# An attention and state-space kernel on one core: the row maxima of the loop turned by VectorE's 32x32 blocks in place of a TensorE transpose

## The chip, the cores and the metric

The kernel runs on one core of a Trainium2 chip. TensorE (PE) multiplies, VectorE (DVE), ScalarE (ACT) and GpSimd (POOL) work element by element, SyncE (SP) issues DMAs. The metric is the device time of one execution in microseconds, the median over runs.

## The reference, cut to what matters

Two independent heads are computed in float32 and put side by side. Head A is a long convolution (a kernel made of 256 complex exponentials per channel, applied through Fourier transforms). Head B is full softmax attention with 16 heads of 28 channels over 2048 positions:

```python
x = inputs["B_x"]            # (1, 2048, 448); u has the same shape
qkv = (x @ wqkv).reshape(B, S, 3, H, Dh).transpose(2, 0, 3, 1, 4)
scores = einsum("bhqd,bhkd->bhqk", q, k) * Dh ** -0.5
o = einsum("bhqk,bhkd->bhqd", softmax(scores), v)
b = o.transpose(0, 2, 1, 3).reshape(B, S, D) @ wo
a = irfft(rfft(u, 2L) * rfft(K, 2L))[:L] + u * D_skip   # K = 2 Re sum_n C exp(A dt l)
return concatenate([a, b], -1)
```

## The kernel before, in words

Attention works in 16 rows: row u is one group of four heads (`g = u // 4`) and one chunk of 512 queries (`c = u % 4`). A row has 16 key tiles of 128 keys; one key tile is one step of the loop (lines 1061 to 1118), 256 steps in all. The softmax needs each query's maximum before its exponentials, so a row's maxima are computed a row and three steps ahead (`LEAD`): while step s multiplies, exponentiates and sums row u, it also makes four products (`m0` to `m3`, function `max_mm`) for the maxima of the next row. DVE reduces them from PSUM into `mx`; for one of the four, ACT first makes `rl` and DVE adds and reduces in one custom operation.

The maximum enters the scores as two more channels of q. The tile `qhat` holds q with every channel on four partitions (high and low parts), and K has ones in its channels 28 and 29 (`kones`). When the sixteenth step of a row's maxima is done, `max_join` reduces `mx` to `m1`, 128 queries by 16 numbers (4 heads by 4 tiles of 128 queries). `max_end` (lines 214 to 220) splits them into minus the maximum rounded to fp32r and the rest, `max_put` (222 to 225) writes them by DMA into partitions 112 and 116 of `qhat`. Since `m1` has queries on partitions and the row in `qhat` has them along one partition, they have to be turned: `nc.tensor.transpose` does so into a PSUM tile `pm`, and the pair of DVE operations reads it there as 16 partitions of 128.

The order in which a step's work is written is a table, `ORDER` (line 35); every engine executes its own instructions in the order written. Letters `m` and `s` are products for the maxima and for the scores, `pv` the sums with V, `v` one DVE operation of head A, `k` head A's kernel blocks, `f` a slot. There are two slots a step (three at the end), one before `pv` and one behind it; each takes the first job that is due: urgent ones (`soon_slot`), then the others: `u_stage1` and `u_stage2` (products `ua`), blocks of head A's kernel (`e,g` and `w,ko`), spectra (`yk,mw` and `p,mw`), the last transform (`zi,wb`), output projections (`ua,og`). The turn of a row's maxima is an urgent job, due two slots after the join (line 1116). All these jobs and the products for the maxima share three PSUM tiles `pm` in a ring: the next user of a tile waits until DVE or ACT has emptied it.

GpSimd's work in the loop is `e_power` (lines 689 to 701): per block of head A nine products or sums on SBUF tiles `e`, `eu`, `sdb`, in three sizes. DVE's own share, `g_powers` (703 to 726), keeps one operand `zg` in PSUM. SP issues all DMAs of the loop, in the order written.

Row 0's maxima are made before the loop in a stage of their own (lines 603 to 605).

Of the kernel before, what the change touches and what calls it, by code (L numbers as in the profile page):

```python
# [21 lines left out]
DH = 28  # L22
G = 4
HG = H // G
CQ = 512
NQ = L // CQ
NK = L // 128
# [13 lines left out]
UG = (2, 2, 4)  # L41
# [51 lines left out]
def body(ctx, tc, a, out):  # L93
    nc = Engines(tc)
# [23 lines left out]
    ident = const.tile([128, 128], F32, name="ident")  # L118
# [37 lines left out]
    def load_v(g, c):  # L156
        v_g[g, c] = t = v_p.tile([128, NK // NQ, HG, 32], F32, name="v", bufs=5)
        nc.sync.dma_start(t.rearrange("p t h e -> p t (h e)"), v_d[c][:, g])

    def load_kd(g, j, rows=range(4)):  # L160
        if 0 in rows:
            kd_g[g, j] = kd_p.tile([128, CQ], F32R, name=f"kdif{j}")
        t = kd_g[g, j]
        for r in rows:
            nc.sync.dma_start(t[r::4].bitcast(F32), kd_d[g][r % 2, 32 * j:32 * j + 32, :])

    def load_q(u, rows=range(4)):
        g, c = divmod(u, NQ)
        if 0 in rows:
            q_u[u] = q_p.tile([128, HG, CQ], F32R, name="qhat", bufs=3)  # L170
        t = q_u[u]
        for r in rows:
            nc.sync.dma_start(t[r::4].bitcast(F32), q_d[g][c][r // 2].rearrange("(j p) q -> p j q", j=HG))
# [36 lines left out]
    def max_join(u, n=3):  # L210
        m_u[u, 1] = q_p.tile([128, HG * 4], F32, name="m1", bufs=2)
        nc.vector.tensor_reduce(m_u[u, 1], m_u[u].rearrange("p a b c -> p (a b) c")[:, :, :n], axis=AX.X, op=ALU.max)

    def max_end(u, ps):
        nc.tensor.transpose(ps[:16, :128], m_u[u, 1], ident)
        mh = q_p.tile([16, 2, 128], F32R, name="mh")
        nc.vector.tensor_scalar(mh[:, 0, :], ps[:16, :128], -1.0, None, op0=ALU.mult)
        nc.vector.scalar_tensor_tensor(mh[:, 1, :], ps[:16, :128], -1.0, mh[:, 0, :].bitcast(F32),
                                       op0=ALU.mult, op1=ALU.subtract)
        mh_u[u] = mh  # L220

    def max_put(u, queue=nc.sync):
        for i in range(2):
            queue.dma_start(q_u[u][4 * (DH + i):4 * (DH + i) + 1, :, :].rearrange("p h (t q) -> p (h t) q", t=4).bitcast(F32),
                                mh_u[u][:, i, :].bitcast(F32))


    with ExitStack() as st:
        sst, xst, wst = ExitStack(), ExitStack(), ExitStack()
# [5 lines left out]
        ps_t = pool(st, "ps_t", 2, PSUM)  # L235
# [25 lines left out]
        t = a["A_log_dt"]  # L261
# [51 lines left out]
        for s in (1, 0, 2):  # L313
            for k in range(NCK):
                for p in range(1 if k < NCK - 1 else 2):
                    n = CK if k < NCK - 1 else TL
# [284 lines left out]
        nc.scalar.activation(half_pi[:1], half_pi[:1], AF.Exp)  # L601
        n_st.close()
        max_join(0, 2)
        max_end(0, ps_t.tile([128, CQ], F32, name="pt"))
        max_put(0, nc.scalar)
        sst.close()


# [160 lines left out]
    def s_mm(u, kt, j):  # L769
        pss = ps_s.tile([128, CQ], F32, name="pss")  # L770
        nc.tensor.matmul(pss, kt_g[u // NQ][j][:, kt * 128:(kt + 1) * 128], q_u[u][:, j, :], start=True, stop=True)
        p = kq_p.tile([128, CQ], F32, name="p", bufs=PB)
        nc.scalar.activation(p, pss, AF.Exp, scale=SCALE)
        return p
# [10 lines left out]
    def load_og(u):  # L785
        og_u[u] = og = kq_p.tile([128, G - 1, CQ], F32, name="og")
        nc.sync.dma_start(og, on_d[u % NQ][:G - 1].rearrange("g p q -> p g q"))
# [217 lines left out]
    def soon_slot(gap, f):  # L1005
        n_urgent[0] += 1
        urgent.append((n_slot[0] + gap, n_urgent[0], f))
        q = sorted(urgent)
        urgent.clear()
        urgent.extend(q)  # L1010

    def slot(s_):
        n_slot[0] += 1
        if urgent and urgent[0][0] <= n_slot[0]:
            urgent.popleft()[2]()
        elif s_ >= NS and f_slot(s_, "s"):
            pass
        elif p_due and p_due[0][0] <= s_:
            p_due.popleft()[1]()
        elif m_due and m_due[0][0] <= s_:  # L1020
            m_due.popleft()[1]()
        elif u_due and u_due[0][0] <= s_:
            u_part(*u_due.popleft()[1:])
        else:
            f_slot(s_, "s") or f_slot(s_, "f")

    def k_seed(s_):
        b = k_due[0] if k_due else NB
        if b < NB and b not in egs and done["mm"] >= b - 2 and K0 + b * KP <= s_ + (1 if b in es else 2):
            k_seeds(b)  # L1030
# [30 lines left out]
    for s in range(NS):  # L1061
        u, kt = divmod(s, NK)
        sm = s + NK + LEAD
        if s == 12 * NK:
            k0_st.close()
            f_p["s", 0] = f_p["s", 1] = pool(f0_st, "f0_p", side="right")
            f_ready["s", 0], f_ready["s", 1] = s, NS
        if s >= 12 * NK and f_ready["s", 1] == NS and not (k_due or m_due or powers["g"] or powers["e"]):
            g_st.close()
            ps_st.close()  # L1070
            ps_w[:] = pool(ps_st, "ps_f", 4, PSUM), 1
            f_ready["s", 1] = s + F1
        if kt == 12 and u // NQ == G - 1:
            load_og(u)
        late[0] = s + NK + LEAD > NS
        if u % NQ == NQ - 1 and u < NU - 1 and kt % 4 == 2:
            load_v(u // NQ + 1, kt // 4)
        if sm < NS and sm // NK % NQ == NQ - 1 and sm % NK % 4 == 0 and sm % NK and sm // (NQ * NK) + 1 < G:
            load_kd(sm // (NQ * NK) + 1, sm % NK // 4 - 1)
        if sm < NS and sm % (NQ * NK) == 0 and sm:  # L1080
            load_kd(sm // (NQ * NK), HG - 1)
        if kt % 4 == 1 and u % NQ == 1 and u // NQ + 1 < G:
            load_k(u // NQ + 1, kt // 4, k_pools[(u // NQ + 1) % 2])
        if kt == 2:
            if u + 2 < NU:
                load_q(u + 2)
        ps = []
        for op in ORDER:
            if op[0] == "s":
                ps.append(s_mm(u, kt, int(op[1])))  # L1090
            elif op[0] == "f":
                slot(s)
            elif op[0] == "v":
                vec()
            elif op == "k":
                k_next()
                k_begin(s)
                k_seed(s)
                for _ in range(3):
                    if powers["e"]:  # L1100
                        powers["e"].popleft()()
            elif op == "pv":
                if prev:
                    pv_step(*prev)
                    if prev[1] == NK - 1:
                        fin(prev[0], s)
            elif sm < NS:
                max_mm(sm // NK, sm % NK, int(op[1]))
        for _ in range(FX if late[0] else 0):
            slot(s)  # L1110
        if sm < NS and sm % NK == NK - 1:
            def end(un=sm // NK):
                max_end(un, w_tile())
                max_put(un)
            max_join(sm // NK)
            soon_slot(UG[0], end)
        k_next()
        prev = (u, kt, ps)
    pv_step(*prev)
# [65 lines left out]
```

## Time and profile before

| what | us |
|---|---|
| median of 3 runs | 1278.05 (1277.69 to 1278.42) |
| the profiled execution | 1278.83 |
| its span, first to last instruction | 1277.0 |
| PE busy | 1216.2 |
| ACT busy | 967.0 |
| DVE busy | 922.6 |
| POOL busy | 843.6 |

A row of a timeline gives the start and the length in us, the engine, the operation, what it writes and reads, its shape, and in brackets how long the engine had been idle and who ended that. A group's row gives a count, the busy time and the mean in ns, then the idle time before it. All lines stand as L77, a helper through which every operation is recorded, so tiles tell them apart: `pm` and `pss` are PSUM tiles, `po` the sums with V, `mh` the split maxima. The loop lies between about 230 and 1252 us.

### The profile page before, as it was taken

Reading aid. Unit: us, or ns where it says so; the run is one execution under the profiler, and the core shown is the slowest. Engines: PE = TensorE matmul, PEld = TensorE weight load, DVE = VectorE, ACT = ScalarE, POOL = GpSimd, SP = SyncE. Lnnn points to the kernel's source line nnn. Section 1 sums busy time; section 2 is a strip of 40 time slices with the busy share of each in tenths; the row PEclk is TensorE's granted clock in tenths of the full one; section 3 lists DMA queues with packets and bytes.
Section 4 is the critical chain, followed back from the end, with each engine's and each line's share of the span. In section 5 each row is a group of like instructions: output and inputs, shape, how many; then the busy total and the mean of one; then the engine's idle time right before and its main releaser. Section 6 shows DMA issues by size and latency. Waiting matters only on the chain.

```text
span 1277.0 us, 33251 instructions
## 1 busy us (share of the span) xinstructions
PE 1216.2 (95%) x12593; PEld 692.5 (54%) x12593; DVE 922.6 (72%) x2106; ACT 967.0 (76%) x2162; POOL 843.6 (66%) x728
## 2 busy tenths in 40 slices
PE   6788888999999999999999999999999999999998
PEld 4666764555555555555555555555555555544433
DVE  5788966877777877778778988888887645645111
ACT  5888865788888888888888888888887656656552
POOL 2666740798788888878689999989995222324321
PEclk9999898899999999999999999999999999999999
DMA  6678789436554645475533133432224533657656
GB/s 194 211 258 290 275 278 359 124 88 187 159 154 114 169 118 159 123 224 177 171 101 96 57 80 105 145 91 71 83 60 149 171 139 135 205 162 237 203 163 174
DMA packets 203528, 206.22 MB, mean 161 GB/s; under 512 B 98344, under 2 KB 162408, under 8 KB 201320
## 3 DMA queue, kind: packets, MB, share of 16 engines
q1 hardware_dynamic: 202840, 203.50, 51.8%
q8 instruction: 99, 1.62, 0.5%
q10 hardware_dynamic: 528, 0.59, 0.2%
q14 instruction: 61, 0.50, 0.1%
HBM read 121.60 MB, written 82.18 MB: 160 GB/s over the span
## 4 chain that ended last, share of the span: by engine, by line
PE 79%; DVE 9%; ACT 5%; issue 3%; POOL 2%; DMA 1%; SPq 1%; ACTq 0%; POOLq 0%; DVEq 0%
PE pm L77 44%; PE pss L77 17%; PE po L77 17%; DVE tri L77 1%; ACT tri L77 1%; DVE mx L77 1%; DVE sg L77 1%; SPq L77 1%; ACT rl L77 1%; DVE hl L77 1%; DVE px L77 1%; ACT p L77 1%; PE pt L77 1%; POOL p L77 1%; DVE g L77 1%
## 5 line engine op out<-in xcount | busy, mean ns | idle before, releaser
L77 ACT ACTIVATE p<-pss 128x512 f32<-128x512 f32 x1024 | 561.3, 611 | 111.5 <-PE pss L77 108.4
L77 PE MATMUL pss<-qhat,khat 128*128 128x512 f32 x1024 | 402.8, 399 | 1.5 <-ACT p L77 1.4
L77 DVE TENSOR_REDUCE mx<-pm 128x1 f32<-128x512 f32 x480 | 308.3, 683 | 108.9 <-PE pm L77 106.8
L77 PE MATMUL pm<-khat,qhat 128*128 128x512 f32 x749 | 326.3, 439 | 6.6 <-ACT rl L77 4.4
L77 POOL TENSOR_TENSOR e<-e,sdb 128x256 f32<-128x256 f32 x168 | 201.8, 1201 | 111.4 <-ACT e L77 62.2
L77 PE MATMUL po<-p,v 128*32 128x512 f32 x2048 | 269.1, 594 | 0.0
L77 POOL TENSOR_TENSOR e<-e,eu 128x256 f32<-128x256 f32 x168 | 248.1, 1477 | 13.2
L77 PEld LDWEIGHTS pm<-khat,qhat 128*128 128x128 f32 x749 | 141.2, 189 | 202.8 <-ACT p L77 46.9
L77 DVE CUSTOM_DVE_ANT_0 rl<-pm,rl 128x512 f32<-128x512 f32 x259 | 178.2, 688 | 73.7 <-ACT rl L77 70.8
L77 PEld LDWEIGHTS pss<-qhat,khat 128*128 128x128 f32 x1024 | 190.4, 188 | 46.1 <-issue 10.8
L77 POOL TENSOR_TENSOR eu<-e,sdb 128x256 f32<-128x256 f32 x168 | 201.9, 1202 | 0.0
L77 POOL TENSOR_TENSOR p<-pr,pr 64x448 f32<-64x448 f32 x64 | 73.1, 1142 | 161.4 <-PE pm L77 134.7
L77 ACT ACTIVATE rl<-pm 128x512 f32<-128x512 f32 x259 | 156.8, 607 | 15.4 <-PE pm L77 9.4
L77 DVE TENSOR_TENSOR g<-g,zg 128x128 f32<-128x128 f32 x392 | 161.9, 413 | 3.4
L77 PE MATMUL pm<-kdif,qhat 128*128 128x512 f32 x249 | 100.9, 405 | 6.0 <-DVE xn L77 4.1
L77 PE MATMUL pm<-xh,khat 128*128 128x512 f32 x256 | 85.0, 423 | 12.1 <-DVE hl L77 5.3
L77 DVE TENSOR_TENSOR zg<-g,zg 128x128 f32<-128x128 f32 x224 | 88.0, 393 | 5.0
L77 PEld LDWEIGHTS pm<-e,g 128*32 128x32 f32 x3584 | 57.2, 109 | 43.9 <-issue 16.2
L77 DVE TENSOR_TENSOR pr<-pm,ub 128x448 f32<-128x448 f32 x64 | 37.0, 619 | 56.4 <-PE pm L77 42.0
L77 PE MATMUL pm<-e,g 128*32 128x64 f32 x3584 | 73.0, 222 | 1.9 <-POOL e L77 1.3
L77 ACT ACTIVATE y<-pm 128x448 f32<-128x448 f32 x48 | 26.5, 553 | 58.2 <-PE pm L77 35.9
L77 ACT ACTIVATE ub<-pm 128x224 f32<-128x224 f32 (+1 forms) x96 | 38.7, 448 | 39.5 <-PE pm L77 37.4
(135 smaller groups left out, 1436.7 us busy)
## 6 DMA issues: line engine op xcount, KB each, us to landing
sdb<-sd SPq DMA_DIRECT2D x55, 336.0 KB
qhat<-q SPq DMA_DIRECT2D x64, 256.0 KB
khat<-k SPq DMA_DIRECT2D x64, 256.0 KB
sd<-sg SPq DMA_DIRECT2D x8, 1456.0 KB
k<-hl SPq DMA_DIRECT2D x16, 512.0 KB
mw<-in_mw SPq DMA_DIRECT2D x16, 512.0 KB
sd<-qhat SPq DMA_DIRECT2D x8, 896.0 KB
yu_d<-ub SPq DMA_DIRECT2D x64, 112.0 KB
```

The source lines that it names most:

```text
L77: i = f(*args, **kw)
```

## The change

`max_end` no longer uses TensorE. Straight behind the join, DVE takes the rounded negative and the rest on `m1` as it lies, 128 partitions by 16 (into `mh`, now an SBUF tile of 128 by 2 by 16), and then turns that tile of 128 by 32 with its own transpose, which turns each block of 32 partitions by 32 elements by itself (into `mt`). In `mt`, 32 partitions hold the two parts of 16 numbers for 32 queries, so `max_put` needs four requests, one for each block, with pieces of 32 elements, in place of two with pieces of 128. The urgent job is gone from the slots. Row 0 keeps the old way (`max_first`).

```diff
-    def max_end(u, ps):
-        nc.tensor.transpose(ps[:16, :128], m_u[u, 1], ident)
-        mh = q_p.tile([16, 2, 128], F32R, name="mh")
-        nc.vector.tensor_scalar(mh[:, 0, :], ps[:16, :128], -1.0, None, op0=ALU.mult)
-        nc.vector.scalar_tensor_tensor(mh[:, 1, :], ps[:16, :128], -1.0, mh[:, 0, :].bitcast(F32),
-                                       op0=ALU.mult, op1=ALU.subtract)
-        mh_u[u] = mh
-
-    def max_put(u, queue=nc.sync):
-        for i in range(2):
-            queue.dma_start(q_u[u][4 * (DH + i):4 * (DH + i) + 1, :, :].rearrange("p h (t q) -> p (h t) q", t=4).bitcast(F32),
-                                mh_u[u][:, i, :].bitcast(F32))
+    def max_end(u):
+        m = m_u[u, 1]
+        hl = q_p.tile([128, 2, HG * 4], F32R, name="mh")
+        nc.vector.tensor_scalar(hl[:, 0], m, -1.0, None, op0=ALU.mult)
+        nc.vector.scalar_tensor_tensor(hl[:, 1], m, -1.0, hl[:, 0].bitcast(F32), op0=ALU.mult, op1=ALU.subtract)
+        mh_u[u] = q_p.tile([128, 32], F32, name="mt")
+        nc.vector.transpose(mh_u[u], hl.bitcast(F32).rearrange("p i n -> p (i n)"))
+
+    def max_put(u):
+        row = q_u[u][4 * DH:4 * DH + 8:4].bitcast(F32).rearrange("p h (t b q) -> p (h t) b q", t=4, b=4)
+        for b in range(4):
+            nc.sync.dma_start(row[:, :, b, :], mh_u[u][32 * b:32 * b + 32, :])
...
         if sm < NS and sm % NK == NK - 1:
-            def end(un=sm // NK):
-                max_end(un, w_tile())
-                max_put(un)
             max_join(sm // NK)
-            soon_slot(UG[0], end)
+            max_end(sm // NK)
+            max_put(sm // NK)
```

On DVE, before, at the join of row 9 (`m_11421` is the joined tile, `mx` the maxima of single products, `ISA` the custom operation that makes `rl`):

```order
L77 TENSOR_TENSOR g<-g,zg 128x32x4
L77 TENSOR_REDUCE m_11421<-mx 128x16
L77 ISA rl,mx<-pm_11432,rl 128x512
L77 ISA mx 128x1
L77 TENSOR_TENSOR g<-g,zg 128x32x8
L77 TENSOR_SCALAR mh<-pm_11463 16x128
L77 SCALAR_TENSOR_TENSOR mh<-pm_11463,mh 16x128
L77 TENSOR_TENSOR zg<-g,zg 128x256
L77 TENSOR_REDUCE mx<-pm_11475 128x1
```

And there now:

```order
L77 TENSOR_TENSOR g<-g,zg 128x32x4
L77 TENSOR_REDUCE m_11437<-mx 128x16
L77 TENSOR_SCALAR mh<-m_11437 128x16
L77 SCALAR_TENSOR_TENSOR mh<-m_11437,mh 128x16
L77 STREAM_TRANSPOSE mt<-mh 128x32
L77 ISA rl,mx<-pm_11457,rl 128x512
L77 ISA mx 128x1
L77 TENSOR_TENSOR g<-g,zg 128x32x8
L77 TENSOR_TENSOR zg<-g,zg 128x256
L77 TENSOR_REDUCE mx<-pm_11493 128x1
```

The two operations that read PSUM behind the custom one are now three that read SBUF ahead of it.

On PE, before, the step behind the join of row 2 (`pm_4206` is the turn, `ua,w_111` and `e,g` are slot jobs):

```order
L77 MATMUL po<-p,v 32x512 x4
L77 MATMUL pm_4206<-ident,m_4160 16x128
L77 MATMUL pm_4218<-khat,qhat 128x512
L77 MATMUL pss<-qhat,khat 128x512
L77 MATMUL pm_4225<-khat,qhat 128x512
```

And there now:

```order
L77 MATMUL po<-p,v 32x512 x4
L77 MATMUL pm_4217<-ua,w_111 32x448 x4
L77 MATMUL pm_4237<-khat,qhat 128x512
L77 MATMUL pss<-qhat,khat 128x512
L77 MATMUL pm_4244<-khat,qhat 128x512
```

The slot that held the turn takes a `ua` job that stood in a later step. This is so in rows 2, 3, 4 and 6; in rows 1, 5 and 7 to 12 the slot is left out, and from row 13 on the spectrum jobs move up by one slot each time.

More of the change, by code (lines that the diff above doesn't have):

```diff
@@ L212, in max_join, with max_first @@
         nc.vector.tensor_reduce(m_u[u, 1], m_u[u].rearrange("p a b c -> p (a b) c")[:, :, :n], axis=AX.X, op=ALU.max)
-    def max_end(u, ps):
-        nc.tensor.transpose(ps[:16, :128], m_u[u, 1], ident)
-        mh = q_p.tile([16, 2, 128], F32R, name="mh")
+    def max_end(u):
[9 more added lines that the diff above has]
+            nc.sync.dma_start(row[:, :, b, :], mh_u[u][32 * b:32 * b + 32, :])
+    def max_first(ps):
+        nc.tensor.transpose(ps[:16, :128], m_u[0, 1], ident)
+        mh = q_p.tile([16, 2, 128], F32R, name="m0")
         nc.vector.tensor_scalar(mh[:, 0, :], ps[:16, :128], -1.0, None, op0=ALU.mult)
@@ L219, in max_end @@
                                        op0=ALU.mult, op1=ALU.subtract)
-        mh_u[u] = mh
-    def max_put(u, queue=nc.sync):
         for i in range(2):
-            queue.dma_start(q_u[u][4 * (DH + i):4 * (DH + i) + 1, :, :].rearrange("p h (t q) -> p (h t) q", t=4).bitcast(F32),
-                                mh_u[u][:, i, :].bitcast(F32))
+            nc.scalar.dma_start(q_u[0][4 * (DH + i):4 * (DH + i) + 1, :, :].rearrange("p h (t q) -> p (h t) q", t=4)
+                                .bitcast(F32), mh[:, i, :].bitcast(F32))
     with ExitStack() as st:
@@ L603, in body @@
         max_join(0, 2)
-        max_end(0, ps_t.tile([128, CQ], F32, name="pt"))
-        max_put(0, nc.scalar)
+        max_first(ps_t.tile([128, CQ], F32, name="pt"))
         sst.close()
```

## Prediction

> **What bounds the kernel now.** I read the busy shares, then TensorE's timeline through the attention loop, then DVE and GpSimd in the same microseconds.
>
> ```profile
> PE 1216.2 (95%) x12593; PEld 692.5 (54%) x12593; DVE 922.6 (72%) x2106; ACT 967.0 (76%) x2162; POOL 843.6 (66%) x728
> ```
>
> TensorE is busy 95% of the span, so the loop's length is TensorE's work and whatever stops it. One step of the loop (one key tile) runs from one group of `po` products to the next:
>
> ```profile
> 324.79 1.04 PE L77 MATMUL po<-p,v 128*32 128x512 f32 x8
> ...
> 329.05 1.04 PE L77 MATMUL po<-p,v 128*32 128x512 f32 x8
> ...
> 332.55 1.04 PE L77 MATMUL po<-p,v 128*32 128x512 f32 x8
> ...
> 779.41 1.06 PE L77 MATMUL po<-p,v 128*32 128x512 f32 x8
> ...
> 782.29 0.50 PE L77 MATMUL pm<-khat,qhat 128*128 128x512 f32 x1 [0.20 <-DVE mx L77]
> ...
> 783.42 1.04 PE L77 MATMUL po<-p,v 128*32 128x512 f32 x8
> ```
>
> The step at 329.05 carries one slot job (the `e,g` products) and takes 3.50 us. The step at 324.79 carries a `ua,w` job besides and takes 4.26: a job in a slot costs its own 0.76. The step at 779.41 has the same `e,g` job and, in its second slot, the turn of row 9's maxima: 4.01 us, 0.51 more than without. The bracket says where that goes: the product at 782.29 waited for DVE to empty a PSUM tile. DVE in that step:
>
> ```profile
> 779.57 0.19 DVE L77 TENSOR_REDUCE m<-mx 128x16 f32<-128x48 f32 x1
> 779.68 0.68 DVE L77 CUSTOM_DVE_ANT_0 rl<-pm,rl 128x512 f32<-128x512 f32 x1
> ...
> 780.71 0.28 DVE L77 TENSOR_SCALAR mh<-pm 16x128 fp32r<-16x128 f32 x1
> 781.03 0.28 DVE L77 SCALAR_TENSOR_TENSOR mh<-pm,mh 16x128 fp32r<-16x128 f32 x1
> 781.24 0.41 DVE L77 TENSOR_TENSOR zg<-g,zg 128x256 f32<-128x256 f32 x1
> ```
>
> The pair that splits the maxima holds DVE from 780.71 to 781.24, 0.53 us, and the step grows by 0.51. So DVE has almost no slack in such a step: what is put on it, TensorE pays.
>
> **The change, part by part.** *Removed:* in each of rows 1 to 12 a turn in a slot with its pair on DVE, at row 9's 0.51: 12 x 0.51 = -6.1 us. In rows 2, 3, 4 and 6 a `ua` job moves into the freed slot from a later step; the total of jobs is the same, but that step is now 0.76 longer and gives DVE that much room: 4 x 0.76 = -3.0 of what DVE is late.
>
> *Added on DVE:* three small operations between the join and the next `rl`. The nearest rows are the ones at the start of the program, 56 elements a lane, dependent on each other as these are:
>
> ```profile
> 3.88 0.61 DVE L77 TENSOR_SCALAR sg<-sg 8x56 f32<-8x56 f32 x3 [3.88 <-DMA sg<-in_A_log_dt]
> 4.52 0.45 DVE L77 SCALAR_TENSOR_TENSOR sg<-sg 8x56 f32<-8x56 f32 x2
> ```
>
> Three dependent multiplies take 0.61, so about 0.21 from one to the next; two of the other kind 0.45, about 0.24. The join's 0.19 with the gap behind it is 0.23. No row shows a block turn; between 0.1 (the join is over for the independent operation behind it 0.11 after its start) and 0.28 (the 128-element pair above) I take 0.12, nearer the join, since it has 32 elements a lane. Together 0.80 from the join's start to `rl`, against 0.11 now: 0.69 later. `rl` mostly waits for ACT anyway:
>
> ```profile
> L77 DVE CUSTOM_DVE_ANT_0 rl<-pm,rl 128x512 f32<-128x512 f32 x259 | 178.2, 688 | 73.7 <-ACT rl L77 70.8
> ```
>
> 73.7 us of idle over 259 is 0.28 each, which hides that much: 12 x (0.69 - 0.28) = +4.9 (between +3 and +7 by the turn's bounds). The Trainium skill, “VectorE: DVE Perf Modes”, section “The three transpose paths”, gives 311 ns for DVE on 128x128 bf16; with that for the turn, an estimate, the sum would be 2.3 us longer.
>
> *Added, and the largest term:* where these operations read. The old pair read PSUM. The new negation reads and writes SBUF, and the subtraction reads two operands from SBUF. GpSimd's operations read SBUF too, and early in this trace the two engines meet:
>
> ```profile
> 69.67 1.43 DVE L77 TENSOR_SCALAR tri<-tri 128x1232 f32<-128x1232 f32 x1
> ...
> 71.32 1.95 DVE L77 TENSOR_TENSOR tri<-tri 128x1232 f32<-128x1232 f32 x1
> ...
> 89.40 0.38 DVE L77 TENSOR_TENSOR px<-qhat 128x112 f32<-128x112 f32 x1
> 89.69 0.79 DVE L77 TENSOR_SCALAR tri<-tri 128x1232 f32<-128x1232 f32 x1
> ...
> 90.69 1.43 DVE L77 TENSOR_TENSOR tri<-tri 128x1232 f32<-128x1232 f32 x1
> ...
> 141.72 1.09 DVE L77 TENSOR_TENSOR px<-qhat 128x112 f32<-128x112 f32 x1
> ```
>
> ```profile
> 69.42 1.02 POOL L77 TENSOR_TENSOR x_e<-qhat 128x336 f32<-128x336 f32 x1
> 70.52 1.46 POOL L77 TENSOR_TENSOR qhat<-qhat,x_e 128x336 f32<-128x336 f32 x1
> ...
> 141.57 1.02 POOL L77 TENSOR_TENSOR qhat<-qhat 128x336 f32<-128x336 f32 x1 [1.04 <-DVE qhat L77]
> ```
>
> The SBUF-to-SBUF multiply takes 0.79 with GpSimd idle (89.69) and 1.43 when it starts at 69.67 inside a GpSimd operation that ends at 70.44: it ends 0.66 after that. The product behind it (71.32) is then held by the next GpSimd operation, up to 71.98: 1.95 instead of 1.43. A 112-element product of two SBUF operands takes 0.38 alone and 1.09 at 141.72, ending 0.22 after GpSimd does at 142.59. So a DVE operation of these two kinds waits for the whole GpSimd operation that was there first, and two in a row let one GpSimd operation in between. In the loop GpSimd does nearly nothing but these, nine per block, in threes from the smallest up:
>
> ```profile
> L77 POOL TENSOR_TENSOR e<-e,eu 128x1024 f32<-128x1024 f32 x56 | 133.6, 2386 | 4.4
> L77 POOL TENSOR_TENSOR eu<-e,sdb 128x1024 f32<-128x1024 f32 x56 | 107.2, 1915 | 0.0
> L77 POOL TENSOR_TENSOR e<-e,sdb 128x1024 f32<-128x1024 f32 x56 | 107.2, 1914 | 4.4
> ...
> L77 POOL TENSOR_TENSOR e<-e,eu 128x512 f32<-128x512 f32 x56 | 72.9, 1303 | 4.4
> L77 POOL TENSOR_TENSOR eu<-e,sdb 128x512 f32<-128x512 f32 x56 | 59.3, 1059 | 0.0
> L77 POOL TENSOR_TENSOR e<-e,sdb 128x512 f32<-128x512 f32 x56 | 59.3, 1058 | 4.4
> L77 POOL TENSOR_TENSOR e<-e,eu 128x256 f32<-128x256 f32 x56 | 41.5, 742 | 4.4
> L77 POOL TENSOR_TENSOR eu<-e,sdb 128x256 f32<-128x256 f32 x56 | 35.4, 632 | 0.0
> L77 POOL TENSOR_TENSOR e<-e,sdb 128x256 f32<-128x256 f32 x56 | 35.3, 631 | 102.6 <-ACT e L77 62.2 <-DMA sdb<-sd 39.8
> ```
>
> ```profile
> 228.00:985.00 757.00, 752.17 (x8937) 419.36 (x8937) 622.08 (x1478) 632.13 (x1445) 650.07 (x510) 1.00 0.44 125
> 97.40:100.70 3.30, 3.30 (x11) 2.91 (x10) 2.71 (x6) 3.14 (x7) 3.00 (x5) 0.50 1.04 351
> ```
>
> POOL is busy 650 of the 757 us between 228 and 985. An operation of length d met at a random moment has d/2 left; over the nine, 56 x (sum of d squared = 18.3) / 2 / 757 = 0.68 us, idle time counted. That is the negation's wait. The next one in line, which then holds the subtraction, is on average 56 x (sum of neighbours' products = 16.4) / 757 = 1.21. Together 1.89 us a row, 12 x 1.89 = +22.7. Row 9 is a bad one:
>
> ```profile
> 779.55 1.92 POOL L77 TENSOR_TENSOR eu<-e,sdb 128x1024 f32<-128x1024 f32 x1
> 781.55 2.39 POOL L77 TENSOR_TENSOR e<-e,eu 128x1024 f32<-128x1024 f32 x1
> ```
>
> Its negation would come at 779.80, wait 1.67 until 781.47, and the subtraction another 2.39. In row 7 DVE has room for it:
>
> ```profile
> 667.08 0.28 DVE L77 TENSOR_SCALAR mh<-pm 16x128 fp32r<-16x128 f32 x1 [2.06 <-PE pm L77]
> ```
>
> It idles 2.06 there, which swallows that row's 1.9: -1.9. Rows 13 to 15 lie behind 985, where the nine forms are done (their 652 us are the 650 of the window); I cost them at nothing. Their freed slots shift the spectrum jobs by a slot, which I put between -1.5 and +1.5.
>
> *The requests:* four in place of two, and SP waits for DVE's turn before it can issue what stands behind them (`yk`, `khat`, `sdb`).
>
> ```profile
> L77 SPq DMA_DIRECT2D qhat<-mh x30: 547/579/1485, 282.1 to 1171.5; - x30
> ```
>
> At 0.58 each, 2.3 us to issue, 1.2 more than now. The row is due three steps after the join, 3 x 3.5 = 10.5 us; join to last issue is 0.69 + 1.89 + 2.3 = 4.9. The 5.6 us left hide it: nothing on the path. No row shows the landing of 128-byte pieces; if that took over 5.6, TensorE would wait at the row's first `pss`.
>
> *Sum:* -6.1 + 4.9 + 22.7 - 3.0 - 1.9 = +16.6. The profiled execution took 1278.83 (span 1277.0), 0.8 over the median of 1278.05, so 1295.4 by its own time and **1294.6** against the median; I say 1294.5.
>
> What carries most is whether the negation too is held, for it writes fp32r, which no SBUF-to-SBUF row here does. By the Trainium skill, “VectorE: DVE Perf Modes”, section “What auto-detection actually checks”, a single source and a destination in SBUF with even outer sizes suffice for the two-port mode, whatever the 4-byte type; by that rule the sum stays as it is. For the subtraction, the Trainium skill, “SBUF — State Buffer”, section “Who interferes with whom”, speaks against the change: two SBUF inputs contend with any GpSimd operation that reads SBUF, and the loser blocks for all of it. The trace agrees (1.09 against 0.38).
>
> **The rivals.** *A, not slower:* operations this short slip in between GpSimd's and wait for none. Then the waits go: 4.9 - 6.1, and in the four rows with a longer step the own 0.41 is hidden: -1.6. Sum -2.8, **1275.3**. For it: none of the rows above has under 100 elements. Against: 112 elements waited. It decides where the wait per row falls under 0.2 us.
>
> *B, half:* only the subtraction is held, or it follows the negation at once without letting GpSimd in: 0.68 a row, 8.1; row 7 hides 0.7. Sum 8.1 + 4.9 - 6.1 - 3.0 - 0.7 = +3.2, **1281.3**. For it: the fp32r question. Against: the pair at 69.67 and 71.32, held one after the other.
>
> *C, the clock falls as well:* after a stop of 3.7 us
>
> ```profile
> 96.80 0.47 PE L77 MATMUL pm<-vh,xh 128*128 128x448 f32 x1 [3.70 <-DVE hl L77]
> ```
>
> the granted clock is 0.50 for the 3.3 us from 97.40 (above), in which nearly half the work is lost, about 1.5 us. Between 228 and 985 it was 1.00 throughout. Waits of 2 to 4 us could do it in four rows, once or twice each: +6 to +9, **1302**. *D:* the row lands late; each us over 5.6 costs 12: 1300 and more.
>
> **How the numbers follow.** Forecast 0.53, A 0.10, B 0.20, C 0.15, D 0.02. The forecast's own range is 1286 to 1301: the waits of twelve rows scatter by some 5 us, the own time by 2, the late slots by 1.5. The range for 8 in 10 is 1281 to 1304: it leaves out A, part of B and the end of C and D. About 0.2%, 2.6 us, is what a measurement of this kernel tells from no change. Faster: 0.07 (most of A). Same: 0.08 (the rest of A, B's lower end). Slower: 0.85.
>
> **What would show it.** In the profile after, in rows 1 to 12: the negation and the subtraction take far over 0.2 us, ending shortly after a GpSimd operation each; the turn is short; the `rl` behind comes 2 us late on average, and a `pm` product waits for it. If both are at 0.15 to 0.25 in every row, A holds; if the negation is short and the subtraction long, B. A PEclk under 9 inside the loop is C; a wait of `pss` for `qhat` at a row's start is D. Wrong altogether if the steps with a join are no longer than their neighbours.

## The result: 1288.5 us, and the profile after

The changed kernel takes 1288.51 us (median of 4 runs, 1287.17 to 1290.57) against 1278.18 before (1277.69 to 1278.42, 4 runs): a ratio of 1.0083, 95% interval 1.0065 to 1.0100, so 10.3 us slower. The forecast was 1294.5 with a range of 1281 to 1304. The direction was right and the wait is the one that was named; 6 us of the forecast did not come. The profiled execution took 1287.91, 9.1 more than the profiled one of before.

From the page, the busy time of each engine:

```profile
PE 1214.1 (94%) x12578; PEld 690.8 (54%) x12578; DVE 936.7 (73%) x2121; ACT 967.5 (75%) x2162; POOL 843.3 (66%) x728
```

TensorE works 2 us less than before (the twelve turns in the loop and three behind it are gone) in a span that is 9 us longer: it stands still more. DVE's busy time grows by 14.1, and that is not own time: the three new operations take 0.56 a row alone (below), as much as the old pair with its 2 x 0.28. The rows below account for 12.8 of it as waits, 12.1 in rows 1 to 12 and 0.7 in row 14. What TensorE waited for in the loop, before (232 to 980) and after (232 to 987), as us in total, times, longest:

```profile
PE pm L77 <- DVE mx L77: 1.9, 10, 0.2
```

```profile
PE pm L77 <- DVE mx L77: 10.1, 13, 2.0
```

The wait is the one that the prediction named, a `pm` product that needs a PSUM tile from DVE, and it grew by 8.2 us. The step of row 9 in TensorE's timeline, to be held against the 4.01 us of before:

```profile
780.11 1.07 PE L77 MATMUL po<-p,v 128*32 128x512 f32 x8
...
783.28 0.50 PE L77 MATMUL pm<-khat,qhat 128*128 128x512 f32 x1 [1.44 <-DVE mx L77]
...
785.80 1.04 PE L77 MATMUL po<-p,v 128*32 128x512 f32 x8
```

It takes 5.69. DVE and GpSimd in that step:

```profile
780.28 0.19 DVE L77 TENSOR_REDUCE m<-mx 128x16 f32<-128x48 f32 x1
780.51 1.63 DVE L77 TENSOR_SCALAR mh<-m 128x16 fp32r<-128x16 f32 x1
782.17 0.18 DVE L77 SCALAR_TENSOR_TENSOR mh<-m,mh 128x16 fp32r<-128x16 f32 x1
782.38 0.21 DVE L77 STREAM_TRANSPOSE mt<-mh 128x32 f32<-128x32 f32 x1
782.52 0.69 DVE L77 CUSTOM_DVE_ANT_0 rl<-pm,rl 128x512 f32<-128x512 f32 x1
```

```profile
778.32 1.92 POOL L77 TENSOR_TENSOR e<-e,sdb 128x1024 f32<-128x1024 f32 x1
780.20 1.91 POOL L77 TENSOR_TENSOR eu<-e,sdb 128x1024 f32<-128x1024 f32 x1
782.18 2.39 POOL L77 TENSOR_TENSOR e<-e,eu 128x1024 f32<-128x1024 f32 x1
```

The negation starts inside a GpSimd operation (`eu`, 780.20) and ends 0.03 after it does (782.14 against 782.11). The subtraction starts at 782.17, just ahead of GpSimd's next operation at 782.18, and is free. All fifteen rows of the three operations, as minimum, median and maximum in ns:

```profile
L77 DVE TENSOR_SCALAR mh<-m x15: 174/175/1630, 278.3 to 1177.3; 128x16 fp32r<-128x16 f32 x15
L77 DVE SCALAR_TENSOR_TENSOR mh<-m,mh x15: 174/552/2289, 278.5 to 1177.5; 128x16 fp32r<-128x16 f32 x15
L77 DVE STREAM_TRANSPOSE mt<-mh x15: 211/211/214, 279.1 to 1177.7; 128x32 f32<-128x32 f32 x15
```

Alone the pair's operations take 0.174 each; the turn is never held. What they take beyond 0.174 is their wait; over rows 1 to 12 that is 12.1 us, where the forecast had 22.7. The 12.1 sit in nine rows: the negation waits in rows 7 and 9 (2.6 us), the subtraction in rows 1, 3, 4, 7, 8, 10, 11 and 12 (9.5 us). Most of the time it is thus the second operation that is held. Row 11, first DVE, then GpSimd:

```profile
896.62 0.17 DVE L77 TENSOR_SCALAR mh<-m 128x16 fp32r<-128x16 f32 x1
896.82 2.28 DVE L77 SCALAR_TENSOR_TENSOR mh<-m,mh 128x16 fp32r<-128x16 f32 x1
```

```profile
896.72 2.35 POOL L77 TENSOR_TENSOR e<-e,eu 128x1024 f32<-128x1024 f32 x1
```

GpSimd's operation starts while the negation runs, 0.1 behind its start. The negation takes its 0.17 all the same, GpSimd's operation is no longer than elsewhere, and the subtraction behind waits until it is over.

One thing more happened in row 11, where the subtraction waited 2.1 us. TensorE's stop, and the windows before, during and after it (the column behind POOL's is the granted clock):

```profile
900.01 0.50 PE L77 MATMUL pm<-khat,qhat 128*128 128x512 f32 x1 [2.00 <-DVE mx L77]
```

```profile
890.00:898.00 8.00, 8.00 (x102) 4.36 (x98) 6.24 (x14) 6.69 (x17) 7.76 (x6) 1.00 0.26 62
898.00:901.50 3.50, 1.30 (x6) 0.77 (x5) 3.43 (x8) 1.31 (x3) 3.34 (x5) 1.00 0.01 1
901.60:905.20 3.60, 3.60 (x27) 1.36 (x27) 2.31 (x6) 2.08 (x5) 3.44 (x4) 0.53 0.19 54
```

After the stop of 2.00 us the clock is at half for 3.4 us: 1.7 us of TensorE's time are lost, once.

### The profile page after: what moved, and what is told of

Same layout as the page of the kernel before. It is cut to its first block, busy times and chain, and to the rows that moved or that the text cites. A ratio compares the mean times of both kernels' runs of the same rounds, so it can differ in the third digit from the quotient of the medians.

```text
span 1286.1 us, 33259 instructions
## 1 busy us (share of the span) xinstructions
PE 1214.1 (94%) x12578; PEld 690.8 (54%) x12578; DVE 936.7 (73%) x2121; ACT 967.5 (75%) x2162; POOL 843.3 (66%) x728
## 4 chain that ended last, share of the span: by engine, by line
PE 76%; DVE 10%; POOL 5%; issue 3%; ACT 3%; DMA 2%; ACTq 0%; SPq 0%; POOLq 0%; DVEq 0%
PE pm L77 42%; PE pss L77 16%; PE po L77 16%; DVE tri L77 2%; DVE mx L77 1%; POOL qhat L77 1%; POOL e L77 1%; DMA xn<-in_B_x 1%; ACT tri L77 1%; DVE mh L77 1%; DVE rl L77 1%; DVE sg L77 1%; DVE px L77 1%; PE pt L77 1%; ACT rl L77 1%
## 5 line engine op out<-in xcount | busy, mean ns | idle before, releaser
L77 PEld LDWEIGHTS pm<-e,g 128*32 128x32 f32 x3584 | 57.2, 109 | 43.8 <-issue 16.4
L77 PEld LDWEIGHTS po<-p,v 128*32 128x32 f32 x2048 | 54.8, 110 | 24.1 <-issue 19.4
```

Of the source, the lines that this page charges most:

```text
L77: i = f(*args, **kw)
```

## The experiments

Three theories. **1, waits for GpSimd:** the pair reads and writes SBUF, and each of the two may have to wait until a GpSimd operation is over. **2, the place:** anything between the join and the next `rl` makes `rl` late, whatever it waits for. **3, the requests:** four on SP in place of two hold up what stands behind them. The table gives the median time, the ratio to the kernel before measured beside it, the waits of the pair in rows 1 to 12 (beyond 0.174 each), the half-clock stretches in the loop, and the loop's length in the profiled execution, from the start of the first `po` group to that of the 196th.

| kernel | us | ratio (95%) | waits | stretches | loop |
|---|---|---|---|---|---|
| before | 1278.2 | | none | 0 | 745.0 |
| changed | 1288.51 | 1.0083 (1.0065 to 1.0100) | 12.1 | 1 | 754.2 |
| maxima in PSUM | 1278.96 | 1.0005 (0.9996 to 1.0015) | 0.0 | 0 | 744.0 |
| new end in the old slot | 1296.80 | 1.0134 (1.0110 to 1.0159) | 14.6 | 1 | 758.8 |
| pair twice | 1312.23 | 1.0259 (1.0242 to 1.0276) | 26.1 | 7 | 777.4 |
| before, four requests | 1280.42 | 1.0017 (1.0008 to 1.0026) | none | 0 | 745.0 |
| PSUM and old slot | 1277.78 | 0.9997 (0.9988 to 1.0006) | 0.0 | 0 | 744.7 |
| one operation between | 1290.96 | 1.0101 (1.0087 to 1.0115) | 12.1 | 1 | 754.3 |
| two operations between | 1300.58 | 1.0177 (1.0162 to 1.0192) | 16.9 | 4 | 764.8 |
| changed, GpSimd short | 1282.94 | 1.0034 (1.0020 to 1.0049) | 0.1 | 3, at the loop's start | 746.2 |
| before, GpSimd short | 1283.20 | 1.0043 (1.0028 to 1.0057) | none | 3, at the loop's start | 748.1 |
| PSUM, late rows in the slot | 1277.44 | 0.9994 (0.9985 to 1.0003) | 0.0 | 0 | 744.0 |
| pair on GpSimd | 1276.97 | 0.9995 (0.9986 to 1.0005) | none | 0 | 742.8 |
| pair on GpSimd, late rows in the slot | 1276.09 | 0.9985 (0.9976 to 0.9994) | none | 0 | 742.6 |

Behind the loop five of these traces have one half-clock stretch more, which the table leaves out: maxima in PSUM, pair twice, one and two operations between, and pair on GpSimd. Each follows a stop of 1.75 to 2.69 us in which TensorE waits for GpSimd's `p`.

### The maxima in PSUM

```
+        if 0 < u < 13:
+            m_u[u, 1] = zgs[max(zgs)][:, Z_G:Z_G + HG * 4]
+        else:
             m_u[u, 1] = q_p.tile([128, HG * 4], F32, name="m1", bufs=2)
```

> The changed kernel (1288.5 us), but for rows 1 to 12 the join of the two halves writes its 16 maxima a lane into spare columns of PSUM instead of SBUF. Same operations, same order, same four requests. Theory 1 (waits for GpSimd, because the negation reads and writes SBUF and the subtraction reads two SBUF operands): no negation and no subtraction of these rows is over 0.3 us any more, rl starts about 0.8 us after the join in every one of them, 11 to 13 us go, and the kernel takes 1275 to 1278, level with the kernel before or a little faster. Theory 2 (the place: whatever stands between the join and the next rl makes rl late): nothing is changed in the place, 1287 to 1290. Theory 3 (the four requests on SP): 1287 to 1290 too.

The same operations in the same order, and 9.6 of the 10.3 us are gone. The pair's rows:

```profile
L77 DVE TENSOR_SCALAR mh<-zg x12: 174/174/175, 279.6 to 949.2; 128x16 fp32r<-128x16 f32 x12
L77 DVE SCALAR_TENSOR_TENSOR mh<-zg,mh x12: 174/174/175, 279.8 to 949.4; 128x16 fp32r<-128x16 f32 x12
```

In none of twelve rows does either wait, though GpSimd works as before. Place and requests are unchanged, so theories 2 and 3 cannot be what costs 10 us. 1279.0 is a little over the 1275 to 1278 that was expected: the loop is 1.1 shorter than before, while the late part, from the start of the 196th `po` group to that of the last, is 278.7 against 275.2. In it TensorE waits once for 2.07 us for GpSimd's `p`, with a half-clock stretch behind it; before, no wait for `p` is over 0.8.

### The new end in the old slot

```
         if sm < NS and sm % NK == NK - 1:
+            def end(un=sm // NK):
+                max_end(un)
+                max_put(un)
             max_join(sm // NK)
-            max_end(sm // NK)
-            max_put(sm // NK)
+            soon_slot(UG[0], end)
```

> The changed kernel, but its new end of a row (negation, subtraction, block turn, requests) is put back where the old one stood, two slots later, instead of right behind the join. Theory 1 (waits for GpSimd): the three operations meet GpSimd's as often there, only at another moment; the mean of negation and subtraction stays far over 0.2 us each, and the kernel takes 1284 to 1291. Theory 2 (the place): 1275 to 1279, with short operations or with long ones that nobody waits for. Theory 3 (the requests): 1287 to 1290.

Theory 2, by which this place would have been some 10 us cheaper, falls: it is 8 dearer. Theory 1 holds in kind, while its number was too low by 6:

```profile
L77 DVE TENSOR_SCALAR mh<-m x15: 167/586/1839, 279.4 to 1180.6; 128x16 fp32r<-128x16 f32 x15
L77 DVE SCALAR_TENSOR_TENSOR mh<-m,mh x15: 174/548/1832, 280.0 to 1181.0; 128x16 fp32r<-128x16 f32 x15
```

Here the negation waits in ten of twelve rows, and often the subtraction as well: 14.6 us. The profiled execution is the fastest of the four (1291.41; the others 1295.79 to 1299.13, at a mean clock of 0.979 to 0.981 against its 0.983), so some of the rest is probably further half-clock stretches; the other three have no trace that would show it.

### The pair twice

```
+        ml = q_p.tile([128, 2, HG * 4], F32R, name="ml")
+        nc.vector.tensor_scalar(ml[:, 0], m, -1.0, None, op0=ALU.mult)
+        nc.vector.scalar_tensor_tensor(ml[:, 1], m, -1.0, ml[:, 0].bitcast(F32), op0=ALU.mult, op1=ALU.subtract)
```

> The changed kernel with the pair made twice: ahead of negation and subtraction, a negation and a subtraction of the same maxima into a tile that nobody reads, in all rows. Theory 1 (waits for GpSimd): the second pair meets another GpSimd operation in most of rows 1 to 12, about 1.0 of wait and 0.36 of its own each: 10 to 17 us on top, 1298 to 1306. If only own time counts (theories 2 and 3): 12 x 0.36, 4 to 5 us on top, 1292 to 1294.

(The second pair stands behind the first, not ahead of it.) It adds 23.7 us. The waits double, 12.1 to 26.1, which is 14.0; the own time of the second pair is at most 12 x 0.36 = 4.3; and six more half-clock stretches lose 6 x 1.7 = 10.2. (One of the stretches is twice as long and counts as two.) The sum, 28.5, is 4.8 more than what came. Of that, 1.9 is waits and own time that overlap: over the twelve rows `rl` comes 16.4 later in all, not 18.3. Part of the rest is room in the rows (row 3's `rl` came 1.0 later and its step grew by 0.8, row 7's 0.8 and 0.4); what is left is not placed. Theory 1 holds, and its price was set too low because the clock was left out. The clock in the last third of the loop:

```profile
760.00:1010.00 250.00, 238.60 (x2792) 134.94 (x2784) 216.26 (x503) 197.74 (x445) 209.08 (x163) 0.97 0.31 91
```

### Four requests in the kernel before

```
-            queue.dma_start(q_u[u][4 * (DH + i):4 * (DH + i) + 1, :, :].rearrange("p h (t q) -> p (h t) q", t=4).bitcast(F32),
-                                mh_u[u][:, i, :].bitcast(F32))
+            row = q_u[u][4 * (DH + i):4 * (DH + i) + 1, :, :].rearrange("p h (t q) -> p (h t) q", t=4).bitcast(F32)
+            for b in range(2):
+                queue.dma_start(row[:, :, 64 * b:64 * b + 64], mh_u[u][:, i, 64 * b:64 * b + 64].bitcast(F32))
```

> The kernel before with each of the two requests of a row split in two, so four requests of 256-byte pieces where there were two of 512. Nothing else. Theory 1 (waits for GpSimd): no effect, 1276 to 1280. Theory 3 (four requests hold SP, and what stands behind them on SP comes late): most of the 10 us of the change, 1284 to 1290.

2.0 us, but not in the loop, which is 745.0 long with and without. Of the 1.5 us between the two profiled executions, 1.2 lie on the way to the first `po` group, 234.69 against 233.50: row 0 is split here too, and its requests go out just ahead of the loop. From row 0's join to the next `rl` it is 7.03 us here and 4.99 to 5.20 in every other trace, and the half-clock stretch that lies there in all of them is 13.65 us long in place of 10.24. The changed kernel leaves row 0 at two requests. Theory 3 falls for the loop. The pieces here are of 256 bytes; those of 128 bytes in the changed kernel are covered by the first experiment, which keeps them.

### PSUM and the old slot

The two edits above together.

> The version with the new end of a row in the old slot (1296.8 us), but with the maxima of rows 1 to 12 in PSUM. Theory 1 (waits for GpSimd): the waits go here too, all 15 to 18 us of them, and the kernel takes 1276 to 1281. Theory 2 (the place): it has the place that was 8 us dearer than behind the join, so it stays over 1285.

```profile
L77 DVE TENSOR_SCALAR mh<-zg x12: 166/169/175, 279.6 to 949.7; 128x16 fp32r<-128x16 f32 x12
```

The place that was 8 us dearer is 1.2 us cheaper by the medians once the maxima don't come from SBUF; the intervals of the two ratios overlap, so that much is not shown. In the traces the loop is 0.7 longer than with the maxima in PSUM alone, and the late part shorter: 276.0 against 278.7. In the loop, without the waits, the place is worth less than a microsecond.

### GpSimd's operations cut short, in both kernels

```
-            nc.gpsimd.tensor_tensor(t[:, :, :, m:2 * m], t[:, :, :, :m], zr, ALU.mult)
+            nc.gpsimd.tensor_tensor(t[:, :, :1, m:2 * m], t[:, :, :1, :m], zr, ALU.mult)
...
+                nc.vector.memset(e2[b], 0.0)
```

The same cut in the two other operations; the two buffers of `e` are filled with zeros once.

> The changed kernel with GpSimd's nine operations of each block cut to one head in sixteen (the other fifteen parts of the spectrum's powers are left out, so the kernel computes only part of its output): as many operations, but GpSimd's rows become short. The pair still reads and writes SBUF. Theory 1 (waits for GpSimd): no negation and no subtraction of rows 1 to 12 is over 0.4 us, and against the kernel before with the same cut it takes between 3 us less and 2 us more. Any theory in which the place, the own time or the requests cost the 10 us: still 8 to 12 more than the kernel before with the cut.

> The kernel before with the same cut of GpSimd's nine operations (it leaves out the same fifteen sixteenths of the powers). All theories: TensorE paces the loop, so 1270 to 1278; it is there to be compared with the changed kernel so cut.

This takes away the other party and leaves the pair in SBUF. In the changed kernel so cut:

```profile
PE 1219.2 (95%) x12578; PEld 694.4 (54%) x12578; DVE 928.7 (72%) x2123; ACT 966.3 (75%) x2162; POOL 321.3 (25%) x728
```

```profile
L77 DVE TENSOR_SCALAR mh<-m x15: 174/176/880, 288.4 to 1174.2; 128x16 fp32r<-128x16 f32 x15
L77 DVE SCALAR_TENSOR_TENSOR mh<-m,mh x15: 174/175/176, 288.6 to 1174.4; 128x16 fp32r<-128x16 f32 x15
```

The one long negation (0.880) is row 14's, where GpSimd runs the spectrum's uncut operations. The two kernels are 0.3 us apart, and in the loop the changed one is 1.9 shorter. Both are 5 us slower than the 1270 to 1278 that was expected, alike, around the loop's first steps: there each loses three half-clock stretches (5.1 us), between 232 and 251, behind stops of TensorE of 2.5 and 2.2 us. Why the cut and the filled buffers lead to those stops was not looked into; it drops out of the comparison.

### One and two operations between join and negation

```
+        if 0 < u < 13:
+            z = zgs[max(zgs)][:, Z_G:Z_G + 32]
+            nc.vector.tensor_scalar(z[:, :16], zgs[max(zgs)][:, :16], 1.0, None, op0=ALU.mult)
+            nc.vector.tensor_scalar(z[:, 16:], z[:, :16], 1.0, None, op0=ALU.mult)
```

(With one, the last line is absent.) The question is why 12 us of waits came and not 23: did the moment count?

> The changed kernel (1288.5 us) with one more small operation, from PSUM to PSUM, between the join and the negation of rows 1 to 12: the pair starts about 0.2 us later against GpSimd's operations, whose order and times stay. If the moment at which the pair meets GpSimd is the same in each run and row by row as in the trace (the phase): by the GpSimd rows of the changed kernel, shifted by 0.21, the waits of the twelve rows add up to 17.0 us instead of 12.2, because the negation is now held in rows 1, 3, 4, 8, 11 and 12, and where it got in free in rows 2 and 5 the subtraction is held; with 12 x 0.21 of its own that is 1294 to 1298. If the moment is random, the waits stay at 12 and only the own time is added: 1290 to 1292.

With one, nothing moved. DVE in row 1:

```profile
278.88 0.20 DVE L77 TENSOR_REDUCE m<-mx 128x16 f32<-128x48 f32 x1
279.00 0.18 DVE L77 TENSOR_SCALAR zg<-zg 128x16 f32<-128x16 f32 x1
279.12 0.18 DVE L77 TENSOR_SCALAR mh<-m 128x16 fp32r<-128x16 f32 x1
279.33 0.62 DVE L77 SCALAR_TENSOR_TENSOR mh<-m,mh 128x16 fp32r<-128x16 f32 x1
```

The independent operation slips into the gap in which the negation waits for the join's result, so the pair starts 0.24 after the join's start by these rows, as without it (0.23 or 0.24). The run fails as a shift, but it is a repetition: the waits are again 12.1, and row by row they differ by no more than 0.05 from those of the changed kernel. Its loop is as long, too (754.3 against 754.2); the 2.5 us by which its median is higher lie, in its trace, in the late part (278.9 against 276.6, with a stop of 2.53 us for GpSimd's `p` and a half-clock stretch behind it), so that its time falls where the random moment was to put it, but not for that reason. The moment is not random. With two the pair does move:

> The changed kernel with two small operations from PSUM to PSUM, the second dependent on the first, between the join and the negation of rows 1 to 12. With one, it slipped into the gap behind the join and moved nothing; with two the pair starts 0.45 after the join in place of 0.23. Phase: the waits add up to 17 us in place of 12.2 (the negation is held in rows 1, 3, 4, 8, 10, 11 and 12, the subtraction in 2, 5 and 10); with 12 x 0.22 of its own 1294 to 1298. Random moment: 12 us of waits as now, 1290 to 1292.

```profile
L77 DVE TENSOR_SCALAR mh<-m x15: 164/646/2301, 278.0 to 1187.6; 128x16 fp32r<-128x16 f32 x15
L77 DVE SCALAR_TENSOR_TENSOR mh<-m,mh x15: 174/177/2201, 278.7 to 1187.8; 128x16 fp32r<-128x16 f32 x15
```

The medians have changed places: 0.2 us later it is mostly the negation that is held. The waits are 16.9 us where 17.0 were worked out. Row by row it is not as close: in row 12 the negation got in, though a GpSimd operation had started 0.01 before it, and the subtraction waited; in rows 8 and 11 the subtraction waits 0.4 besides. The time is above the 1294 to 1298 expected, because three more stops reach 2 us and take the clock along: 4.7 of waits, 12 x 0.19 = 2.3 of own time (the pair starts 0.42 after the join, not 0.45) and 3 x 1.7 = 5.1 are 12.1 over the changed kernel, and 12.1 were measured. That it fits to the tenth is luck: in the traces the loop is 10.6 longer, and 1.5 lie in the late part, which has a half-clock stretch of its own. The clock behind row 4's stop:

```profile
470.00:477.50 7.50, 5.37 (x69) 2.54 (x62) 5.87 (x14) 4.51 (x14) 7.33 (x5) 1.00 0.50 167
477.50:481.00 3.50, 3.50 (x12) 2.26 (x16) 2.51 (x6) 2.17 (x4) 3.26 (x5) 0.52 0.11 32
```

### Versions that might beat both

First, rows 13 to 15 back in the slot, on top of the maxima in PSUM:

```
+            def end(un=sm // NK):
+                max_end(un)
+                max_put(un)
+            if sm // NK < 13:
+                end()
+            else:
+                soon_slot(UG[0], end)
```

> The version with the maxima of rows 1 to 12 in PSUM (1278.96 us), and rows 13 to 15 end in the slot two slots later, as they did in the kernel before, so that the spectrum's jobs keep their old slots there. If the shifted slots cost what the late part grew by in the traces (275.2 us before, 278.7 with the maxima in PSUM, from step 196 to the last), 1275 to 1277.5: faster than the kernel before by 1 to 3. If that growth was scatter of one execution, 1278 to 1280.

The late part is 276.1 us, as against 278.7 without the edit (275.2 before). The longest wait for `p` is 0.8 again, and no half-clock stretch follows. The median is 1.5 lower, but the intervals of the two ratios overlap; it is level with the kernel before. Then the pair on GpSimd, which has it in its own queue:

```
-        nc.vector.tensor_scalar(hl[:, 0], m, -1.0, None, op0=ALU.mult)
-        nc.vector.scalar_tensor_tensor(hl[:, 1], m, -1.0, hl[:, 0].bitcast(F32), op0=ALU.mult, op1=ALU.subtract)
+        nc.gpsimd.tensor_scalar(n, m, -1.0, None, op0=ALU.mult)
+        nc.gpsimd.tensor_scalar(hl[:, 0], m, -1.0, None, op0=ALU.mult)
+        nc.gpsimd.tensor_tensor(hl[:, 1], n, hl[:, 0].bitcast(F32), ALU.subtract)
...
+        if sm < NS + 1 and sm % NK == 0 and sm // NK > 1:
+            max_turn(sm // NK - 1)
+            max_put(sm // NK - 1)
```

> The changed kernel with the pair moved from DVE to GpSimd (three small operations there, in its own queue, so nobody waits for a port), and the turn on DVE with the four requests at the end of the next step. Theory 1: DVE keeps only the turn, the waits go, and the kernel takes 1273 to 1278; if GpSimd is still behind its longest operations when the turn comes, DVE waits for it in a row or two and it is 1277 to 1282. If the place or the requests cost, 1284 and more.

The loop is 2.2 us shorter than before; the time is level with it. In three rows (8, 9 and 11) the work on GpSimd now makes its own next result late, and TensorE waits for that, 2.6 us in all; row 11:

```profile
902.12 0.65 PE L77 MATMUL pm<-e,g 128*32 128x64 f32 x32 [1.17 <-POOL e L77]
```

Last, this with rows 13 to 15 in the slot, their pair on DVE:

> The version with the pair on GpSimd (1276.97 us), and rows 13 to 15 end in the slot two slots later with their pair on DVE, so that the spectrum's jobs keep the slots that they had in the kernel before. If the shifted slots cost what the late part grew by in that version's trace (277.5 us against 275.2 before), 1274 to 1276, faster than the kernel before by 2 to 4 us; if that growth was scatter, 1276 to 1278.

1276.09 against 1278.25 measured beside it: 0.9985, with an interval that leaves out 1 (0.9976 to 0.9994). Of the versions tried it is the only one whose interval lies below 1, by 2 us, which is less than the 0.2% that the prediction took for measurable.

## Why the prediction was right, and where it was off

**TensorE paces, DVE has no slack, the turn costs 0.51.** Held. The twelve steps with a turn were 5.9 us longer before than their jobs account for (0.5 to 0.6 each, 0.2 in row 7), where 6.1 was forecast; that is gone.

**Own time of the three operations, +4.9, less the rows with a longer step.** Held in the mean. The no-wait chain is 0.80 from the join to `rl` (row 13 after: 0.79), and the turn is 0.211, held by nothing, inside the 0.1 to 0.28 that bounded it. With the waits gone, the loop is 1.1 shorter than before (maxima in PSUM) or 1.9 (GpSimd short). The two terms -6.1 and +4.9 give 1.2; rival A, which took off another 1.6 for the rows with a longer step, had 2.8. The mean hides that rows 5, 9, 11 and 12 pay 0.7 to 0.9 each with the maxima in PSUM and the four rows with a longer step next to nothing. (The +3 to +7 that was given for this term doesn't follow from the turn's bounds: 0.1 for the turn gives +4.7.)

**The negation is held although it writes fp32r.** Held: 1.63 in row 9 against 0.174, and 0.174 in each row where GpSimd is out of the way or the input is in PSUM. The Trainium skill, “SBUF — State Buffer”, section “Who interferes with whom”, has it that a two-port operation or one with two SBUF inputs blocks for the whole of the other engine's instruction and that the order of issue decides who blocks. The runs agree: each wait ends 0.03 to 0.04 after GpSimd's operation.

**The waits, +22.7: the step that failed.** The prediction took the pair to arrive at a random moment, and let GpSimd put one operation between the two each time. Both are wrong, and they made 22.7 of what was 12.1: the negation's 8.1 of it came out at 2.6, the subtraction's 14.5 at 9.5. The rows from which the second was taken, 69.67 and 71.32, aren't two in a row either: a product that reads PSUM stands between them at 71.02. First, the moment is fixed: in ten of twelve rows a GpSimd operation ends within 0.3 of where the pair starts, and does so again in the second traced execution of the same order (one operation between). Second, whether GpSimd gets in between depends on its own next operation. If that needs the result of the one that ends, it starts 0.07 to 0.08 later (782.11 to 782.18), and the subtraction behind a held negation, 0.06 after that end, is in first, as in row 9; if not, it starts 0.04 before the end (780.24 to 780.20), and the subtraction waits once more, as in row 7. Where GpSimd's operation ends just ahead of the negation or in its first 0.11, the negation costs nothing, but the next one starts before the subtraction does and holds it: rows 1, 3, 4, 8, 10, 11 and 12, with 9.1 of the 12.1. Row 2 of the kernel before shows that this could have been read there, first GpSimd, then DVE:

```profile
342.88 1.91 POOL L77 TENSOR_TENSOR eu<-e,sdb 128x1024 f32<-128x1024 f32 x1
344.87 2.39 POOL L77 TENSOR_TENSOR e<-e,eu 128x1024 f32<-128x1024 f32 x1
```

```profile
344.41 0.19 DVE L77 TENSOR_REDUCE m<-mx 128x16 f32<-128x48 f32 x1
```

The negation would start at 344.64, wait for the end at 344.79, which costs it nothing, and let the subtraction start at 344.85, ahead of 344.87: no wait, where the average had 1.9. In the changed kernel row 2 waits 0.02. Row 9, the prediction's own example: negation held from 779.80 to 781.50, subtraction at 781.53, ahead of 781.55; 1.5 us and not 1.67 + 2.39. The trace after has 1.46. Done so for all twelve rows, with the rows of before alone, the sum is 12.8; row 8 comes out 0.5 too high, since its GpSimd operation starts 0.06 ahead of the pair before and 0.02 behind it after. This was worked out with the result at hand; the run with two operations between, whose 17.0 was worked out before it ran, is the blind test of it. Why GpSimd's operations stand so to the joins was not tried.

**Row 7 swallows its wait, and four rows give room.** The first held: row 7 waits 1.5, and its step takes 4.84 against 4.88 before. The second hardly mattered, for -3.0 was taken off as if each of rows 2, 3, 4 and 6 had a wait to hide: rows 2 and 6 have next to none, row 3's 0.45 is hidden, and of row 4's 2.1 all but 0.3 lengthens its step.

**Rival C, the clock.** It came once, in row 11, at 1.7 us lost, beside the forecast and not in its place. In the loop of six traces (the changed kernel, the pair twice, the old slot, one and two operations between, the maxima in PSUM), 13 of 15 stops of 2.0 to 3.9 us were followed by a half-clock stretch, and none of the stops up to 1.99. That is no sharp threshold: stops of 2.02 and 2.38 brought none, and behind the loop one of 1.75 brought one. The stretches of a trace all begin a whole number of 3.413 us apart (the changed kernel's at 219.17 and 901.83 lie 200 of them apart), so where a stop falls in that grid may decide; it was not tried. The Trainium skill, “TensorE: Matmul & The Clock Gate”, section “Why this matters for your kernels”, warns of idle gaps over about 3 us; here 2.00 was enough, and the measurement decides.

**Rival A, slipping in, and B, half.** A needs operations too short to be held; 16 elements a lane were held. B has one wait a row at random, 8.1 us of waits, which is nearer to 12.1 than the forecast's 22.7, though its time of 1281.3 is further off than 1294.5. What came has one wait in most rows, by another way: not because the second always follows at once, but because mostly one of the two is free.

**Requests and late rows.** Nothing of the requests on the path in the loop, as forecast. The late part grew by 1.4, at the end of the ±1.5 that was given. Most of it is one longer wait for GpSimd's `p` among the shifted spectrum jobs, which stand one step earlier now: TensorE waits for `p` 3.9 us in all in the late part, against 2.7. First before, then after:

```profile
1179.77 0.96 PE L77 MATMUL pm<-p,mw 128*32 128x224 f32 x16 [0.68 <-POOL p L77]
1182.19 0.96 PE L77 MATMUL pm<-p,mw 128*32 128x224 f32 x16 [0.78 <-POOL p L77]
```

```profile
1185.61 0.96 PE L77 MATMUL pm<-p,mw 128*32 128x224 f32 x16 [1.81 <-POOL p L77]
1188.03 0.96 PE L77 MATMUL pm<-p,mw 128*32 128x224 f32 x16 [0.80 <-POOL p L77]
```

**The sum, and luck.** Between the two profiled executions the loop is 9.2 longer and the late part 1.4; the stage ahead of the loop is 1.6 shorter, though nothing was changed in it (the first `po` group starts between 231.5 and 233.6 in the eleven traces in which that stage is the same). In the terms of the prediction the loop comes out as -1.1 for turns and own time, +12.1 of waits, -3.6 of them hidden (the loop is 8.5 longer for its waits than with the maxima in PSUM) and +1.7 of clock. The forecast had -1.2, +22.7, -4.9 and nothing. That the time lies only 6 us under the forecast, with 10.6 less of waits, is partly luck: the clock, the late part and the smaller share that was hidden made up for 4.5 of it. With 12.1 for the waits and all else as forecast, the sum would have been +6.0 and the time 1284, 4.5 too low.

## What to carry to other kernels

Before an operation is moved from PSUM to SBUF, or from TensorE to DVE, look where its operands lie and what GpSimd does at that moment: an operation on 16 elements a lane waited up to 2.1 us here, and with the maxima in PSUM neither of the two waited. Where both engines repeat the same pattern in each round, don't average over moments: lay the operation's start against the other engine's rows, round by round, for tenths of a microsecond decide between 0 and 2 us. And count a stop of TensorE of about 2 us or more nearly twice, since here in most cases 1.7 us went with the clock behind it.

## What was not expected of the hardware

- GpSimd's next operation starts 0.07 to 0.08 after the last if it needs its result, and 0.04 before the recorded end if it doesn't. That 0.1 decides whether a DVE operation behind a held one gets in.
- An independent DVE operation of 0.18 placed between two dependent ones costs nothing: the pair behind it starts 0.23 to 0.24 after the join with it and without.
- On GpSimd negation and subtraction of 16 elements a lane, one after the other in its queue, take 0.22 to 0.27 each by its rows, against 0.17 on DVE alone.
- A negation on DVE during which a GpSimd operation starts is not held and doesn't hold it: 0.175 and 2.35 to 2.37 us in rows 4, 8 and 11.
- Stops of TensorE of 2.00 to 2.13 us were enough for a half-clock stretch of 3.4 us, in five of six cases in the loops of six traces.
